# Moving the first load of the output projection ahead of the first K load in a one-token decode layer

## The chip, the cores and the metric

The kernel runs on one core of a Trainium2 chip. The core has five engines that run side by side and meet only through semaphores: TensorE (PE, matrix products; its weight loads are listed as PEld), VectorE (DVE), ScalarE (ACT), GpSimd (POOL) and SyncE (SP), which here issues all the loads. Sixteen DMA engines move the data between the chip's memory (HBM) and the core's own memory (SBUF).

The metric is the device time of one execution in microseconds (us), lower is better. A time that is quoted without more is the median of several executions. The profile is of one execution; its span is the stretch from the first to the last instruction of the program, and a little time lies around it.

## What is computed

One token goes through an attention layer with cached keys and values and then through a gated MLP, each with a layer norm in front and a residual sum behind. The batch is 1, the model width 640, there are 32 heads of width 128 and 4096 cached positions. All arrays are bf16.

```python
def _A_ref(x, k_cache, v_cache, wq, wo):
    q = (x @ wq)                                # 640 -> 32 heads x 128
    scores = einsum("bhqd,bhkd->bhqk", q, k) * (Dh ** -0.5)
    p = _softmax(scores, axis=-1)               # over 4096 positions
    o = einsum("bhqk,bhkd->bhqd", p, v)
    return o.reshape(B, Sq, Hq * Dh) @ wo       # 4096 -> 640

def _B_ref(x, w_gate, w_up, w_down):
    h = _gelu(x @ w_gate) * (x @ w_up)          # 640 -> 1728
    return h @ w_down                           # 1728 -> 640

h = x + _A_ref(_layernorm(x), k_cache, v_cache, wq, wo)
return h + _B_ref(_layernorm(h), w_gate, w_up, w_down)
```

With one token every number that is read is used once. K and V are 32 MB each (32 x 4096 x 128 x 2 bytes), wq and wo 5.2 MB each, the MLP's weights 6.6 MB: the 84 MB of the page.

## The kernel before

**Pairs.** The 32 heads are handled as 16 pairs, numbered n = 0 to 15. The K rows of a pair are one load of 2048 KB into one of three buffers (`kt`), the V rows one load of 2048 KB into one of three buffers (`vt`). I call them K0 to K15 and V0 to V15.

**PE's work for a pair.** K comes with positions on the partitions, so PE first transposes it: 64 transposes of 128x128 (`pe_transposes`, L230 to L248, matmuls of L244) in eight groups. VectorE and ScalarE copy six and two of the groups out of PSUM into `ksb` (L581 and L551). Then come 64 small products of the transposed K with q (`pe_scores`, L253). ScalarE takes the exponentials and their sums (L564). The product with V (`pe_pv`, L264, 64 matmuls) follows one pair later: in pair n's turn PE does the transposes of n, PV of n - 1, and the scores of n. Five turns of three pairs are a loop on PE (L352 to L377); pair 0 comes before it.

**The start.** SP issues the load of K0, then waits (L523), then issues x and the five parts of wq. PE transposes x (L312), computes the moments of the layer norm (L293), transposes K0, computes q from wq (L327, one part of wq after the other), brings q into columns (L343), and does the scores of pair 0.

**The output projection.** wo is 4096x640 and is used in four groups of eight heads (four pairs), 1280 KB each. A group is loaded into `wo_in` (`load_wo`, L515 to L519). POOL copies it from there into `wo` (L494) when PE has finished the projection that reads the group before; the projection runs in the second pair of each turn (L361 to L365, matmuls of L276). The turns before the first group is complete run the same projection with a row of zeros (`o_row`) against `wo`; so `wo` is cleared at the start (L481 and L483), in two parts, and PE waits for all the clears once, ahead of its loop (L349). The last group is used out of `wo_in` directly, after the loop (L406).

**SP's order of loads.** All loads go out on one queue, in the order in which SP issues them: K0, [wait], x, wq (five parts), K1, V0, and then for n = 1 to 14 K(n+1) and V(n), and V15. Ahead of V5, V8 and V11 it issues groups 0, 1 and 2 of wo, behind V15 group 3, and then the MLP's weights. SP waits ahead of a K load until PE has transposed the pair that last used the buffer (L505), ahead of a V load until the PV of the pair that last used it is done (L511), and ahead of groups 1, 2 and 3 of wo until POOL has copied the group before (L517).

**The wait at the start.** POOL counts its clears on the semaphore `pool`. The first part of `wo` is the eighth. SP waits for a count of 8 (`POOL_BEGUN`, L523) before it issues x and wq. The data of `wo` is not needed by these loads.

**The end.** Behind the loop PE does the last PV, the last projection, the moments of the second layer norm (L293), the gate and up products (L439, 140 matmuls), and the down product (L413) in the order in which the parts of w_down land. A wait of PE for a landing is L168 (`landed`).

Of the kernel before, what the change touches and what calls it, by code (L numbers as in the profile page):

```python
# [10 lines left out]
def kernel(  # L11
# [20 lines left out]
    PE, DVE, ACT, SP, POOL = nc.tensor, nc.vector, nc.scalar, nc.sync, nc.gpsimd  # L32
# [31 lines left out]
    pool = ctx.enter_context(tc.tile_pool(name="all", bufs=1))  # L64
    psum = ctx.enter_context(tc.tile_pool(name="ps", bufs=1, space=bass.MemoryType.PSUM))

    def sb(name, shape, dtype=f32):
        return pool.tile(shape, dtype, name=name, tag=name)
# [4 lines left out]
    wo_t = sb("wo", [P, HG, D], bf16)  # L73
# [74 lines left out]
    S = {n: nc.alloc_semaphore(f"s_{n}") for n in names}  # L148
# [7 lines left out]
    def spare(engine):  # L156

        i = next(spares)
        return engine.memset(spare_t[:, i : i + 1], 0.0)
# [186 lines left out]
    pe_scores(q_sb[:, 0:2], mark_at(0))  # L346
    PE.sem_inc(S["dve_pe"], -N_DVE_T)
    PE.sem_inc(S["act_pe"], -len(ON_ACT) - 1)
    PE.wait_ge(S["pool"], 9)  # L349

    base = done["pe"]
    with PE.Fori(0, TURNS):  # L352
# [28 lines left out]
    def pe_at(n, name):  # L381


        if n == 0:
            return T[0, name]
        turn, i = divmod(n - 1, UN)
        return T[("turn", i), name] + turn * per_turn
# [90 lines left out]
        POOL.memset(e[:], 0.0).then_inc(S["pool"], 1)  # L478
    POOL.memset(o_row[:], 0.0).then_inc(S["pool"], 1)
    POOL.memset(o_spread[:], 0.0).then_inc(S["pool"], 1)  # L480
    POOL.memset(wo_t[:, 0:2], 0.0).then_inc(S["pool"], 1)  # L481
    POOL_BEGUN = 8
    POOL.memset(wo_t[:, 2:], 0.0).then_inc(S["pool"], 1)  # L483

    for _ in range(2):
        spare(POOL).then_inc(S["wo"], 1)
    POOL.wait_ge(S["pe"], T["start", "q"])
    POOL.memset(wd_sb[0 : P - LAST, FULL, :], 0.0).then_inc(S["pool"], 1)
    POOL_COPIED = 10
    for g in range(NP // PG - 1):  # L490
        POOL.wait_ge(S["wo_in"], 16)
        POOL.sem_inc(S["wo_in"], -16)  # L492
# [2 lines left out]
        spare(POOL).then_inc(S["pool"], 1)  # L495
    POOL_ALL = POOL_COPIED + NP // PG - 1

    def load(name, dst, src):  # L500
        SP.dma_start(dst, src).then_inc(S[name], 16)

    def load_k(n):
        if n >= UN:
            SP.wait_ge(S["pe"], pe_at(n - UN, ("T", NG - 1)))  # L505
        src = A_k_cache[0, 2 * n : 2 * n + 2].rearrange("h (p j) d -> (h p) j d", p=HP)
        load(f"k{n % UN}", kt[n % UN][:], src)

    def load_v(n):
        if n >= UN:  # L510
            SP.wait_ge(S["pe"], pe_at(n - UN + 1, "pv"))  # L511
        src = A_v_cache[0, 2 * n : 2 * n + 2].rearrange("h (p j) d -> (h p) j d", p=HP)
        load(f"v{n % UN}", vt[n % UN][:], src)

    def load_wo(g):  # L515
        if g > 0:
            SP.wait_ge(S["pool"], POOL_COPIED + g)  # L517
        src = A_wo[g * HG * P : (g + 1) * HG * P, :].rearrange("(p j) d -> p j d", p=P)
        load("wo_in", wo_in[:], src)  # L519

    load_k(0)

    SP.wait_ge(S["pool"], POOL_BEGUN)  # L523
    load("x", x_row[:], A_x[0, 0].rearrange("(c p) -> c p", p=P))
    for c in range(DC):
        load(f"wq{c}", wq_sb[:, c, :], A_wq[c * P : (c + 1) * P, :])
# [2 lines left out]
    for n in range(1, NP):  # L529
        if n + 1 < NP:  # L530
            load_k(n + 1)
        if n in (5, 8, 11):
            load_wo((n - 5) // UN)
        load_v(n)
    load_wo(NP // PG - 1)
# [82 lines left out]
    for turn in range(TURNS):  # L618
# [14 lines left out]
        for i in range(UN):  # L633
            n = first + i
# [90 lines left out]
```

## Time and profile before

| | |
|---|---|
| time, median of 4 runs | 208.59 us (208.52 to 208.73) |
| the profiled execution: its own time | 208.73 us |
| the profiled execution: its span | 206.9 us |
| mean granted clock of PE over the span | 0.734 |
| read from HBM | 84.23 MB, 407 GB/s over the span |
| PE, share of the span that it is busy | 81% |
| DVE, ACT, POOL | 41%, 23%, 10% |
| issue of K0 | 0.95 us |
| issue of x, of the last part of wq, of K1 | 3.44, about 5.7, 6.21 us |
| issue of wo's group 0, of V5 | 56.94, 58.16 us |
| POOL's clears of `wo` | 2.24 to 3.41 and 3.35 to 6.66 us |

The page has a row of digits for each engine: the span is cut in 40 slices, and a digit is the busy share of a slice in tenths. PEclk is the clock that TensorE was granted, and below it stand the share of the DMA engines and the GB/s that they moved. In rows of the timeline the first two numbers are the start and the length in us, then come the engine, the line of the kernel, the operation, the tiles (out<-in) and how many such instructions are merged; in brackets stands how long the engine sat idle before and what ended that. "PEq L168" there means that PE's sequencer was waiting for a landing. In the table of waits a row is: who waited, for whom, us in total, how many times, the longest.

### The profile page before, as it was taken

Reading aid. Unit: us, or ns where it says so; the run is one execution under the profiler, and the core shown is the slowest. Engines: PE = TensorE matmul, PEld = TensorE weight load, DVE = VectorE, ACT = ScalarE, POOL = GpSimd, SP = SyncE. Lnnn points to the kernel's source line nnn. Section 1 sums busy time; section 2 is a strip of 40 time slices with the busy share of each in tenths; the row PEclk is TensorE's granted clock in tenths of the full one; section 3 lists DMA queues with packets and bytes.
Section 4 is the critical chain, followed back from the end, with each engine's and each line's share of the span. In section 5 each row is a group of like instructions: output and inputs, shape, how many; then the busy total and the mean of one; then the engine's idle time right before and its main releaser. Section 6 shows DMA issues by size and latency. Waiting matters only on the chain. (4 is left out here: it accounts for less than half of the span.)

```text
span 206.9 us, 7741 instructions
## 1 busy us (share of the span) xinstructions
PE 167.8 (81%) x3599; PEld 162.1 (78%) x3599; DVE 85.2 (41%) x199; ACT 48.4 (23%) x99; POOL 19.8 (10%) x22
## 2 busy tenths in 40 slices
PE   0296699795999988689899589998489899986883
PEld 0282599795999987689899589998489799984881
DVE  7492253341536607045524335252416261614330
ACT  0041132311313513032313113132213131310000
POOL 8200100000000006200003500000800000000000
PEclk9999558585679987859685856696967976765555
DMA  6999999999999999999999999999999999999990
GB/s 203 407 431 436 428 428 421 423 424 431 415 437 418 437 415 443 415 439 418 431 419 433 437 418 440 421 425 427 431 431 424 437 418 440 417 407 414 405 350 20
DMA packets 7789, 84.39 MB, mean 408 GB/s; under 512 B 802, under 2 KB 994, under 8 KB 2402
## 3 DMA queue, kind: packets, MB, share of 16 engines
q1 hardware_dynamic: 7778, 84.24, 96.9%
q8 instruction: 8, 0.13, 0.3%
q14 instruction: 3, 0.02, 0.0%
HBM read 84.23 MB, written 0.00 MB: 407 GB/s over the span
## 5 line engine op out<-in xcount | busy, mean ns | idle before, releaser
L244 PE MATMUL tp<-ident,kt 128*128 128x128 bf16 x1024 | 89.3, 272 | 8.3 <-PEq L168 7.4
L244 PEld LDWEIGHTS tp<-ident,kt 128*128 128x128 bf16 x1024 | 86.8, 127 | 9.2 <-issue 8.6
L581 DVE COPY ksb<-tp 128x1024 bf16<-128x1024 bf16 x96 | 63.8, 688 | 59.9 <-PE tp L244 59.6
L551 ACT COPY ksb<-tp 128x1024 bf16<-128x1024 bf16 x32 | 32.4, 1012 | 49.7 <-PE tp L244 49.7
L264 PE MATMUL o<-ex,vt 128*128 128x2 bf16 x1024 | 28.1, 163 | 8.0 <-PEq L168 8.0
L264 PEld LDWEIGHTS o<-ex,vt 128*128 128x128 bf16 x1024 | 27.4, 97 | 8.4 <-issue 8.4
L253 PE MATMUL s<-q,ksb 128*128 128x2 bf16 x960 | 27.0, 164 | 2.4 <-issue 2.4
L253 PEld LDWEIGHTS s<-q,ksb 128*128 128x128 bf16 x960 | 25.9, 99 | 2.5 <-issue 2.5
L494 POOL COPY wo<-wo_in 128x5120 bf16<-128x5120 bf16 x3 | 13.4, 4451 | 111.3 <-POOLq L492 111.3
L564 ACT ACTIVATE ex<-s 64x64 bf16<-64x64 f32 x32 | 7.6, 238 | 67.8 <-PE s L253 67.4
L643 DVE COPY o_raw<-o 128x2 f32<-128x2 f32 x15 | 2.4, 159 | 24.6 <-PE o L264 24.6
L439 PEld LDWEIGHTS tp<-hc,big 128*128 128x128 bf16 x140 | 8.2, 156 | 1.6 <-issue 1.6
L439 PE MATMUL tp<-hc,big 128*128 128x1 bf16 x140 | 8.3, 196 | 1.4 <-issue 1.4
L312 PE MATMUL m<-ident,x_row 5*128 5x5 bf16 x1 | 0.2, 160 | 8.7 <-PEq L168 8.7
L312 PEld LDWEIGHTS m<-ident,x_row 5*128 5x128 bf16 x1 | 0.1, 100 | 8.7 <-issue 8.7
L564 ACT ACTIVATION_READ_ACCUMULATOR ex<-s 64x1 f32 x32 | 6.4, 200 | 0.4
L276 PE MATMUL a<-o_row,wo 128*128 128x1 bf16 x200 | 5.7, 163 | 0.0
L276 PEld LDWEIGHTS a<-o_row,wo 128*128 128x128 bf16 x200 | 5.5, 96 | 0.0
L192 DVE CAST ident_f<-ident 128x128 f32<-128x128 bf16 x1 | 4.6, 4598 | 0.0
L551 ACT ACT_TABLE_LOAD x1 | 1.3, 1283 | 12.6 <-DVE rs_y L211 12.6
L327 PE MATMUL s<-big,xn_bf 128*1 128x512 bf16 x20 | 1.9, 378 | 2.5 <-PEq L168 2.5
L327 PEld LDWEIGHTS s<-big,xn_bf 128*1 128x1 bf16 x20 | 0.5, 81 | 4.1 <-issue 3.9
(97 smaller groups left out, 51.6 us busy)
## 6 DMA issues: line engine op xcount, KB each, us to landing
kt<-in_A_k_cache_dram SPq DMA_DIRECT2D x16, 2048.0 KB, 26.5
vt<-in_A_v_cache_dram SPq DMA_DIRECT2D x16, 2048.0 KB, 29.2
big<-in_A_wq_dram SPq DMA_DIRECT2D x5, 1024.0 KB, 11.3
wo_in<-in_A_wo_dram SPq DMA_DIRECT2D x4, 1280.0 KB, 26.3
big<-in_B_w_gate_dram SPq DMA_DIRECT2D x1, 2160.0 KB, 29.6
big<-in_B_w_up_dram SPq DMA_DIRECT2D x1, 1296.0 KB, 32.5
big<-in_B_w_down_dram SPq DMA_DIRECT2D x1, 1280.0 KB, 15.7
big<-in_B_w_up_dram SPq DMA_DIRECT2D x2, 432.0 KB, 19.9
```

The source lines that it names most:

```text
L192: dve(lambda: DVE.tensor_copy(ident_f[:], ident[:]), False)
L244: inst = PE.transpose(tp_b[g % NBANK][:, b * DH : (b + 1) * DH], kt[slot][:, g * GRP + b, :], ident[:])
L253: inst = PE.matmul(s_ps[:, j, :], lhsT=ksb[g][:, b * DH : (b + 1) * DH], rhs=q2, start=True, stop=True,)
L264: inst = PE.matmul(o_bank[:, 2 * region : 2 * region + 2], lhsT=vt[slot][:, j, :], rhs=e_t[slot][:, j, :], start=(j == 0), stop=(j == NB - 1),
L276: inst = PE.matmul(attn_ps[:, m : m + 1], lhsT=w[:, j, m * P : (m + 1) * P], rhs=o_row[:, j : j + 1], start=False, stop=last and j == HG - ...
L327: inst = PE.matmul(qr_ps[b][32 * r : 32 * r + 1, :], lhsT=xn_bf[:, c : c + 1], rhs=wq_sb[:, c, h * DH : (h + 4) * DH], start=False, stop=( ...
L439: inst = PE.matmul(ps[:, c : c + 1], lhsT=w[:, j, columns(c)], rhs=hc[:, j : j + 1], start=(j == 0 and c == 0), stop=(j == DC - 1), skip_g ...
L494: POOL.tensor_copy(wo_t[:], wo_in[:]).then_inc(S["wo"], 1)
L551: ACT.copy(ksb[g][:], tp_b[g % NBANK][:]).then_inc(S["act_pe"], 1)
L564: inst = ACT.activation(e_t[n % UN][r, :, i], s_ps[r, :, i], AF.Exp, scale=SCALE, accum_out=rs_all[r, 2 * n + i : 2 * n + i + 1],)
L581: DVE.tensor_copy(ksb[g][:], tp_b[g % NBANK][:]).then_inc(S["dve_pe"], 1)
L643: event(DVE.tensor_copy(o_raw[:, 2 * n - 2 : 2 * n], o_bank[:, 2 * i : 2 * i + 2]))
```

## The change

SP issues group 0 of wo first of all, then K0, x and wq, with no wait between them. The load of group 0 that stood ahead of V5 is gone from there; groups 1, 2 and 3 stay. As nothing waits for the first part of the clear any more, POOL clears `wo` in one instruction, and the counts on `pool` that PE and SP wait for are one lower. The work on PE, DVE and ACT and its order are the same.

```diff
@@ PE, ahead of the loop
-    PE.wait_ge(S["pool"], 9)
+    PE.wait_ge(S["pool"], 8)
@@ POOL
-    POOL.memset(wo_t[:, 0:2], 0.0).then_inc(S["pool"], 1)
-    POOL_BEGUN = 8
-    POOL.memset(wo_t[:, 2:], 0.0).then_inc(S["pool"], 1)
+    POOL.memset(wo_t[:], 0.0).then_inc(S["pool"], 1)
...
-    POOL_COPIED = 10
+    POOL_COPIED = 9
@@ SP
+    load_wo(0)
     load_k(0)
-
-    SP.wait_ge(S["pool"], POOL_BEGUN)
     load("x", x_row[:], A_x[0, 0].rearrange("(c p) -> c p", p=P))
     for c in range(DC):
         load(f"wq{c}", wq_sb[:, c, :], A_wq[c * P : (c + 1) * P, :])
@@ SP, in the loop over the pairs
-        if n in (5, 8, 11):
+        if n in (8, 11):
             load_wo((n - 5) // UN)
         load_v(n)
```

## The prediction

> **What bounds the kernel now.** I read the page first, its slices before its totals. PE is busy for most of the span, but at a clock that goes between half and full; the row that does not vary is the DMA row.
>
> ```profile
> span 206.9 us, 7741 instructions
> PE 167.8 (81%) x3599; PEld 162.1 (78%) x3599; DVE 85.2 (41%) x199; ACT 48.4 (23%) x99; POOL 19.8 (10%) x22
> ...
> DMA  6999999999999999999999999999999999999990
> GB/s 203 407 431 436 428 428 421 423 424 431 415 437 418 437 415 443 415 439 418 431 419 433 437 418 440 421 425 427 431 431 424 437 418 440 417 407 414 405 350 20
> ...
> q1 hardware_dynamic: 7778, 84.24, 96.9%
> ```
>
> The reader is to see one queue, q1, that moves 84.24 MB, is at work in every slice but the first and the last, and keeps 415 to 440 GB/s. At 427 GB/s (the window table's figure for 20 to 60 us) 84.24 MB take 197.3 us of the 206.9. So the time is: when the stream starts, how many bytes it has, whether it is ever empty, and what is left to do behind its last byte.
>
> Next I read who waits at the end, PE's timeline from 188 us on:
>
> ```profile
> 192.06 8.25 PE L439 MATMUL tp<-hc,big 128*128 128x1 bf16 x140 [1.42 <-issue]
> ...
> 200.66 0.30 PE L413 MATMUL tp<-big,hid 128*1 128x160 bf16 x4 [0.35 <-PEq L168]
> 201.35 1.24 PE L413 MATMUL tp<-big,hid 128*1 128x160 bf16 x32 [0.38 <-PEq L168]
> 202.88 0.83 PE L413 MATMUL tp<-big,hid 128*1 128x160 bf16 x20 [0.29 <-PEq L168]
> ```
>
> L168 is where PE waits for a landing. The last matmuls wait three times, 1.02 us in all: the final parts of w_down set the end, and PE alone would be at most about 1 us earlier. From the last matmul (203.71) to the span's end it is 3.2 us of copy, store and closing, which the change does not touch.
>
> Then SyncE's own waits, for what the removed wait holds back:
>
> ```profile
> SPq L501 <- POOL wo L481: 2.1, 1, 2.1
> ```
>
> Last, PE around the place that wo's first group leaves:
>
> ```profile
> 76.54 5.22 PE L244 MATMUL tp<-ident,kt 128*128 128x128 bf16 x64 [0.56 <-PEq L168]
> 84.67 1.75 PE L264 MATMUL o<-ex,vt 128*128 128x2 bf16 x64 [2.90 <-PEq L168]
> 86.28 1.83 PE L253 MATMUL s<-q,ksb 128*128 128x2 bf16 x64
> 87.97 0.57 PE L375 MATMUL m<-rs_cur,ones_f 128*128 128x8 f32 x2
> 89.41 5.60 PE L244 MATMUL tp<-ident,kt 128*128 128x128 bf16 x64 [0.87 <-PEq L168]
> ```
>
> K6 landed at 76.5, V5 at 84.6, K7 at 89.4. Between 76.54 and 89.41 three loads landed, 1280 + 2048 + 2048 = 5376 KB in 12.87 us. So a 2048 KB load takes 4.90 us of the stream and a group of wo 3.06 us.
>
> **The change, part by part.**
>
> *The wait removed (SP, 2.1 us).* Behind it stood x and the five wq loads (x issued at 3.44 instead of about 1.35). Do they land sooner? x lands at 8.7 (PE's first matmul, 8.71, waits on L168), only when K0 in front of it has gone through, and wq follows at the stream's rate (wq3 at 18.66, wq4 at 21.14: 2.48 us for 1024 KB). The queue was not empty between 3.4 and 8.7; K0's transfer hides the wait. Gain 0.
>
> *The load moved.* wo's first group (1280 KB, one DMA, issue 0.44 us) goes from behind K6 to the head of SP's order, past 18 issues: K0 to K6, V0 to V4, x and five of wq. Everything it passes lands 3.06 us later; everything from V5 on has the same bytes in front of it as before. Bytes, DMA count and the first issue (0.95 us) stay. If the stream starts equally well, its end stays: 0.
>
> *PE's delay.* x, K0, wq, K1 and K2 land 3.06 later, so PE's first transposes begin near 12.9 instead of 9.80, those of K1 near 29.1 (26.04 + 3.06) and those of K2 near 40.4 (37.37 + 3.06). From K2's transposes to pair 6's PE waits for no load until 75.98; 75.98 - 37.37 = 38.6 us, so PE would be ready for K6 at 79.0, and K6 lands at 79.6. Its transposes end after 5.2 us, at 84.8, when V5 (84.6) is already there. From 84.67 to the end of the totals PE needs 3.87 us, so it is ready for K7 at about 88.7, and K7 lands at 89.4 as before. The 2.90 us wait ahead of PV5 becomes a wait ahead of K6, and the delay is gone by pair 7, with 0.7 us over. Were pair 6's transposes at half clock (6.43 us, the row at 50.11, against 5.22) PE would be 0.5 us late at K7, and the next waits (0.98 us ahead of K8, 2.11 ahead of PV8) take that up. After 89.4 PE has 9.3 us of such waits. Cost 0.
>
> *SP and the buffers.* K3's issue waits for K0's transposes: 16.27 becomes about 19.4. It lands near 50, with K2 and V1 ahead of it in the queue, and the page's median from issue to landing is 26.5 us for kt and 29.2 for vt; 3 us of 26 are cover enough. Cost 0; without that cover, 3 us.
>
> *POOL.* Two clears of wo (1.17 and 3.31 us) become one of about 4.4; PE's wait on it (8 instead of 9) comes at about 29 us, long after 6.7. The first copy of wo_in (4.45 us) no longer waits for the load (79.66) but for pair 5's projection (72.78 + 3.1 = 75.9), so wo's second load is not held back any more: SP's two waits on that copy were 3.3 us, none of which emptied the queue. Four DVE evictions beside the copy took 2.63 us, 0.66 each, against 0.69 without it: no contention. 0.
>
> *The start of the stream.* This is the one term that the trace of before doesn't price. In the window table by single microseconds the stream moves 49, 229, 279 and 393 GB/s in the four from 1 to 5 us; up to 9.0 us it moves 2.58 MB, which is 6.05 us at 427. So 2.95 us are lost: 1.97 before the first packet, 0.98 in a ramp. In the packet records the first packets (16 KB) of K0 took 0.96 to 1.75 us, later ones 0.61, and K0's parts land over 0.77 us (7.85 to 8.62), a spread that later loads keep. The new head has 10 KB packets, and nine more issues follow without a pause. From below: if the ramp goes by packets, 6/16 of 0.98 = 0.37 us are saved, and of the spread 6/16 of 0.77 = 0.29, together -0.6. From above: the ramp is doubled, +1.0. If it goes by time, 0. I take 0, as most of the first packets took over 1 us and the size cannot be told apart here.
>
> Sum: 208.73 (the profiled execution: span 206.9 and 1.8 around it) + 0. The median of the four runs is 208.59, 0.14 lower; I forecast against it: 208.6.
>
> *Rules.* After that sum, two places of the Trainium skill. "DMA: Bandwidth & Descriptors", Anatomy of one DMA, gives a DMA (of the GpSimd path) a fixed cost of about 2.0 us beside bytes / 436 GB/s. By it wo's group would delay K0 by 5.0 us, not 3.06, an estimate against the change. The row above (12.87 us for three loads) leaves no room for fixed costs between queued loads. "TensorE: Matmul & The Clock Gate", Part 1, says that the clock is throttled by default and that activity releases it. The table grants 1.00 from 0 to 20 us with PE busy for 9.09 of 20, and 0.50 from 22 to 30 with PE busy for 6.84 of 8. By the rule the busy catch-up after 40 us would run at full clock; I count it at the clock of its rows.
>
> **The rivals.**
>
> 1. *The start suffers (slower).* The wait also keeps SP from issuing while the engines are starting: only K0's descriptors are there until 3.44. Now wo, K0, x and wq are issued from 0.95 to about 4.3, across the whole ramp (1.97 to 3.9). If that makes it half as long again or twice as long, the end moves by 0.5 to 1.0 us: 209.1 to 209.6, centre 209.3. It decides from a loss above 0.4 us. For it: one engine began its first packet only at 2.89, so the start is uneven. Against it: no row shows issues and packets in each other's way later.
>
> 2. *The start gains (faster).* 10 KB first packets and the smaller spread, -0.4 to -0.6: 208.1. For it: the last landing sets the end, and a late engine stays late. Against it: a slow start may be one of time.
>
> 3. *PE doesn't catch up (slower).* It would have to lose 9.3 us more in waits, or run T2 to T15 at half clock. Beyond that, each us is a us: 210 or more. Against it: the working above.
>
> 4. *It moves 3 us of waiting and nothing else.* This is the forecast.
>
> **How the numbers follow.** The measurement tells about 0.2% from no change, 0.42 us. Forecast, 208.2 to 209.0: 0.43. Rival 1: 0.30. Rival 3: 0.04. Rival 2: 0.23. The range takes in both ends of the start, 208.59 - 0.6 - 0.1 = 207.9 and 208.59 + 1.0 = 209.6, and leaves rival 3 and the far ends of the others out. The forecast's own range is 208.2 to 209.0.
>
> **What would show it.** In the profile after: PE's first matmul near 11.8; transposes of K1 near 29.1; a wait of 2.5 to 3.5 us on L168 ahead of pair 6's transposes and none ahead of its PV; K7's transposes again at 89.4 within 0.5; the last matmuls still with waits on L168. If K7 comes at another time by x, the start of the stream has moved by x, and I expect the end to move with it; the first slices' GB/s say by which rival. If K7's wait on L168 is gone and PE is late from there on, it is rival 3. An empty queue anywhere (a slice under 400 GB/s between 10 and 185 us) would make the whole reading wrong.

## The result and the profile after

| | before | after |
|---|---|---|
| time, median | 208.64 us (60 runs) | 208.27 us (40 runs) |
| ratio, 95% interval | | 0.9983 (0.9978 to 0.9987) |
| the profiled execution: its own time | 208.73 us | 208.31 us |
| the profiled execution: its span | 206.9 us | 206.5 us |

The change makes the kernel faster by 0.37 us, 0.17%. That is small, but nearly four times the half-width of the interval. The forecast was no change; a gain of 0.4 to 0.6 us stood there as rival 2.

The rows of the page that answer to those of before:

```profile
span 206.5 us, 7740 instructions
PE 168.3 (81%) x3599; PEld 162.6 (79%) x3599; DVE 85.3 (41%) x199; ACT 48.4 (23%) x99; POOL 19.8 (10%) x21
...
DMA  5999999999999999999999999999999999999990
GB/s 198 446 413 422 451 409 441 411 435 409 438 419 425 428 435 425 428 427 425 428 422 438 425 428 428 428 424 426 435 425 435 422 428 425 428 406 414 407 360 24
...
q1 hardware_dynamic: 7778, 84.24, 96.8%
```

The bytes are the same, and again there is no empty slice. The first slice is lower than before (198 against 203) and the second higher (446 against 407): a slice is 5.17 us, too coarse for what follows. By single microseconds the window table gives 2.70 MB up to 9.0 us, against 2.58 MB before. Three rows of PE's timeline of the kernel before, to compare with:

```profile
8.71 0.16 PE L312 MATMUL m<-ident,x_row 5*128 5x5 bf16 x1 [8.71 <-PEq L168]
...
26.04 6.52 PE L244 MATMUL tp<-ident,kt 128*128 128x128 bf16 x64 [0.21 <-PEq L168]
...
37.37 6.00 PE L244 MATMUL tp<-ident,kt 128*128 128x128 bf16 x64 [1.53 <-PEq L168]
```

PE's timeline of the kernel after, from its start to the place in the middle and then the end:

```profile
11.51 0.16 PE L312 MATMUL m<-ident,x_row 5*128 5x5 bf16 x1 [11.51 <-PEq L168]
...
28.80 5.15 PE L244 MATMUL tp<-ident,kt 128*128 128x128 bf16 x64 [0.20 <-PEq L168]
...
40.05 6.29 PE L244 MATMUL tp<-ident,kt 128*128 128x128 bf16 x64 [1.10 <-PEq L168]
...
79.20 5.36 PE L244 MATMUL tp<-ident,kt 128*128 128x128 bf16 x64
84.40 1.75 PE L264 MATMUL o<-ex,vt 128*128 128x2 bf16 x64
86.00 1.74 PE L253 MATMUL s<-q,ksb 128*128 128x2 bf16 x64
87.61 0.37 PE L375 MATMUL m<-rs_cur,ones_f 128*128 128x8 f32 x2
88.99 5.36 PE L244 MATMUL tp<-ident,kt 128*128 128x128 bf16 x64 [1.02 <-PEq L168]
...
200.21 0.30 PE L413 MATMUL tp<-big,hid 128*1 128x160 bf16 x4 [0.35 <-PEq L168]
200.93 1.23 PE L413 MATMUL tp<-big,hid 128*1 128x160 bf16 x32 [0.42 <-PEq L168]
202.45 0.84 PE L413 MATMUL tp<-big,hid 128*1 128x160 bf16 x20 [0.29 <-PEq L168]
```

The reader is to compare the starts with those of before. The first matmul is 2.80 us later (11.51 for 8.71), not 3.06; K1's transposes are 2.76 us later (28.80 for 26.04), K2's 2.68 (40.05 for 37.37); K7's transposes come 0.42 us earlier (88.99 for 89.41) with a wait on the landing in both; the last matmuls come 0.43 us earlier (202.45 for 202.88) and still wait for w_down. So the first landing that PE waits for comes 0.26 us earlier than the forecast has it, and the end has gained what K7 has gained.

**The landing records.** For a load into 128 partitions the trace has 16 increments of its semaphore, one per DMA engine, here called landings; each engine has eight packets of such a load. Counted from the first packet of the queue, the last landing of the last load (the last part of w_down, wd3) is at 201.19 us before and 200.74 after. The profiled executions' own times are 7.54 and 7.57 us later, and the same difference is 7.53 to 7.59 in 16 of the 18 profiles of this study (7.80 and 7.87 in e5 and e6). So the time of this kernel is the last landing of wd3 and about 7.56 us.

K1's landings tell the start. Two numbers serve below: the **start loss**, which is the mean of K1's 16 landings less the time that one engine's packets up to there take at their steady durations (0.611 us for 16 KB, 0.385 for 10 KB, 0.309 for 8 KB, so 16 x 0.611 + 40 x 0.309 = 22.14 us for K0, wq and K1), and the **spread**, last less first of the 16.

| | start loss | spread at K1 |
|---|---|---|
| before | 1.56 us | 0.74 us |
| after | 1.34 us | 0.34 us |

What was gained at the start stays. Less the bytes that it has more or less ahead of it, the mean landing is 0.22 us earlier than before at K1, and 0.22 or 0.23 at K7, K15 and V15; for wd3 it is 0.32, and no run shows what the last 0.1 us is. The last of wd3's 16 landings lies 1.11 us behind their mean before and 0.99 after, so the end moved by 0.32 + 0.12 = 0.44 us (0.45 by the rounded times above).

The first packets show where it comes from. Here are six of the first for each kernel (start from the queue's first packet, size, duration):

```
before  0.00 16 KB 1.10   0.06 16 KB 1.53   0.13 16 KB 1.70   0.42 16 KB 1.60   0.92 16 KB 0.86   0.99 16 KB 1.42
after   0.00 10 KB 1.08   0.06 10 KB 1.27   0.08 10 KB 1.23   0.73 10 KB 0.67   0.85 10 KB 0.52   1.07 10 KB 0.39
```

Before, some engines have their first packet done after 1.0 us and others after 2.0, and several second packets are slow too. After, eight packets begin at once and the next eight 0.7 to 1.1 us later, all of these are done by about 1.5 us, and from then on packets take their steady time.

### The profile page after: what moved, and what is told of

Read it like the earlier page. It is cut to its first block, busy times and chain, and to the rows that moved or that the text cites. A ratio compares the mean times of both kernels' runs of the same rounds, so it can differ in the third digit from the quotient of the medians.

```text
span 206.5 us, 7740 instructions
## 1 busy us (share of the span) xinstructions
PE 168.3 (81%) x3599; PEld 162.6 (79%) x3599; DVE 85.3 (41%) x199; ACT 48.4 (23%) x99; POOL 19.8 (10%) x21
## 5 line engine op out<-in xcount | busy, mean ns | idle before, releaser
L244 PE MATMUL tp<-ident,kt 128*128 128x128 bf16 x1024 | 90.3, 274 | 7.2 <-PEq L168 6.6
L244 PEld LDWEIGHTS tp<-ident,kt 128*128 128x128 bf16 x1024 | 87.7, 128 | 8.2 <-issue 7.2
L481 POOL MEMSET wo<- 128x5120 bf16 x1 | 4.4, 4373 | 0.0
```

The costliest lines, as they stand in the source:

```text
L244: inst = PE.transpose(tp_b[g % NBANK][:, b * DH : (b + 1) * DH], kt[slot][:, g * GRP + b, :], ident[:])
L481: POOL.memset(wo_t[:], 0.0).then_inc(S["pool"], 1)
```

## The experiments

The gain could have three causes: the wait that is gone (B), the group's place in the middle (C), and the start of the stream by the first load (A); within A it could be the packets' size or something else in that load. "Ratio" is the time over that of the kernel before, measured beside it. "Start loss" and "spread" are from the one profiled execution of each program.

**e1, the wait alone.** `SP.wait_ge(S["pool"], POOL_BEGUN)` is taken out of the kernel before.

> The kernel before without SP's wait; wo's first group stays ahead of V5, K0 is the first load. Theory A (the size of the first packets sets how far apart the 16 engines start, and the last engine sets the end): K0's 16 KB packets are first as before, so K0's parts land over about 0.8 us as before and the time stays, ratio 0.999 to 1.001. Theory B (the wait's removal made the gain): the spread falls to about 0.4 us and the ratio is 0.998 or less. Theory C (the group's place in the middle matters): ratio 1.000.

Measured: ratio 1.0006 (0.9997 to 1.0015), start loss 1.57, spread 1.09. The wait is worth nothing in time. B falls.

**e2, the move alone.**

```diff
+    load_wo(0)
     load_k(0)
     SP.wait_ge(S["pool"], POOL_BEGUN)
...
-        if n in (5, 8, 11):
+        if n in (8, 11):
```

> wo's first group is first and K0 second, as in the kernel after, but SP's wait stands behind K0 again, ahead of x. Theory A: spread of the first load about 0.4 us, ratio about 0.998. Theory B: no gain, ratio 1.000, spread about 0.8 us. Theory C: ratio about 0.998.

Measured: 0.9985 (0.9976 to 0.9994), start loss 1.36, spread 0.32. It has the whole gain, with the wait still there.

**e3, the group early but not first.** `load_wo(0)` stands behind `load_v(0)`, and not ahead of V5.

> K0 first and SP's wait as before; only wo's first group goes from ahead of V5 to behind V0, early but not first. Theory A: K0's packets start the stream as before, spread about 0.8 us, ratio 0.999 to 1.001. Theory B: 1.000. Theory C (what counts is that PE no longer has the 2.9 us wait in the middle): ratio about 0.998.

Measured: 0.9999 (0.9990 to 1.0008), start loss 1.50, spread 0.84. C falls: taking the group out of the middle gains nothing. It has to be the head of the queue.

**e4, nothing moved, K0 in halves.**

```diff
-    landed("k0")
+    PE.wait_ge(S["k0"], 32)
+    PE.sem_inc(S["k0"], -32)
...
-    load_k(0)
+    half = A_k_cache[0, 0:2].rearrange("h (p j) d -> (h p) j d", p=HP)
+    for i in range(2):
+        part = slice(i * NB // 2, (i + 1) * NB // 2)
+        load("k0", kt[0][:, part, :], half[:, part, :])
```

> The kernel before with K0 loaded by two loads of 1024 KB, so that the first packets have 8 KB in place of 16; wo and the wait as before. Theory A: the spread falls to 0.4 us or less and the ratio to about 0.998, with nothing moved. Theories B and C: ratio 1.000.

Measured: 0.9978 (0.9969 to 0.9987), start loss 1.28, spread 0.75. This has the gain of the change without the change: PE's first matmul is at 8.76, so K0 is not delayed. But the spread, by which theory A explains the gain, did not fall (0.75 against 0.74); the start loss did. The end is earlier all the same:

```profile
200.31 1.67 PE L414 MATMUL tp<-big,hid 128*1 128x160 bf16 x36 [0.35 <-PEq L168]
202.28 0.84 PE L414 MATMUL tp<-big,hid 128*1 128x160 bf16 x20 [0.31 <-PEq L168]
```

These rows of PE's timeline of e4 are the last matmuls, 0.60 us earlier than before and still behind landings.

**e5, K0 in quarters (4 KB packets).**

> The kernel before with K0 in four loads of 512 KB, packets of 4 KB. Theory A2 (each engine's first one or two packets take about 0.5 to 1.1 us longer the more bytes they have, so the size of the first packets sets what the start costs): at least the gain of 8 KB packets, ratio 0.9965 to 0.998; mean of the 16 engines' landings of K0 0.2 to 0.4 us earlier than before. Rival D (what counts is that a second load is queued early, not the packet's size): ratio about 0.998, no better than halves. Rival E (a slow start of fixed time, 8 KB was luck): ratio 0.999 to 1.001.

Measured: 1.0058 (1.0045 to 1.0072), start loss 1.78, spread 1.02. None of the three theories has this; it is the opposite of what "smaller is better" (A2) asks for. A part of it is the packets themselves: four of 4 KB take 0.636 us, one of 16 KB 0.611, so K0 takes 0.20 us more.

**e6, K0 by heads (two loads of 64 partitions).**

> K0 in two loads of 1024 KB like the halves, but cut by head: 64 partitions each, packets of 16 KB as before. Theory A2: no gain, ratio 0.999 to 1.001. Rival D: the gain of the halves, about 0.998.

Measured: 1.0219 (1.0206 to 1.0233). It does not test what it was made for, as its page shows about half the rate in the second slice and more than 400 only from the fourth on:

```profile
GB/s 149 217 290 425 436 427 427 419 424 427 427 421 427 427 423 437 421 436 422 424 437 423 427 433 427 424 433 422 429 430 427 430 427 430 430 404 414 402 362 20
```

**e7, the kernel after with wo's group in two halves (5 KB packets).**

> The kernel after with wo's first group in two loads of 640 KB, packets of 5 KB in place of 10. Theory A2: 0.1 to 0.3 us better than the kernel after, ratio 0.997 to 0.998. Rival D and rival E: as the kernel after, 0.998 to 0.9985.

Measured: 0.9990 (0.9981 to 0.9999), start loss 1.58, spread 0.93. That is no better than the kernel after (0.9983) and outside what A2 forecast, though the intervals of the two overlap. The profiled execution (208.77 us) was the slowest of its runs (median 208.37), so its start loss is rather high for this program.

**e8, K0 as a quarter of 4 KB packets and three quarters of 12 KB.**

> K0 in two loads: first a quarter with 4 KB packets, then three quarters with 12 KB packets. Theory A2: as only the first packets of each engine are slow, the gain is that of the quarters, ratio 0.9965 to 0.998. If the packets of all of K0 mattered, the gain would be smaller than that of the halves, 0.998 to 0.9995.

Measured: 1.0022 (1.0013 to 1.0031), start loss 1.67, spread 1.01. It is slower than before, which neither expectation has.

**e9, K0 cut 40 + 24 blocks (10 and 6 KB); e10, 48 + 16 (12 and 4 KB).**

> The kernel before with K0 in two loads, first 40 of its 64 blocks (packets of 10 KB, as wo's), then 24 (6 KB); nothing moved. Theory A3 (what the start costs depends on the size of the first packets and is least near 8 to 10 KB; the tensor does not matter): as the kernel after, ratio 0.9975 to 0.999. Rival F (wo's rows are what starts well, not their size; the halves had another reason): 0.9995 to 1.001.

> The same with 48 blocks (12 KB) and then 16 (4 KB). Theory A3: between 10 and 16 KB, ratio 0.9985 to 1.0005. Rival F: 1.000 to 1.002 (more, smaller packets).

Measured: e9 1.0026 (1.0016 to 1.0036), start loss 1.62, spread 0.74; e10 1.0019 (1.0010 to 1.0028), start loss 1.91, spread 0.60. Both are slower, e9 by more than rival F has too. With packets of wo's size, cut out of K0, the start is not wo's start (1.62 against 1.34). Theory A3, that the size alone decides, fails in e9. The start does not carry all of e9's time either: the mean of wd3's landings is where it was before, but the last of the 16 is 0.37 us later. One engine is 1.75 us behind the mean in the first load of w_up, against 1.26 before; why is open.

**e11, wq's first part at the head (8 KB packets), wo left in the middle.**

```diff
+    load("wq0", wq_sb[:, 0, :], A_wq[0:P, :])
     load_k(0)
...
-    for c in range(DC):
+    for c in range(1, DC):
```

> The kernel before with the first part of wq (1024 KB, packets of 8 KB, contiguous) ahead of K0; wo stays ahead of V5. Theory A3: the start of the halves, mean start loss about 1.3 us in place of 1.56, ratio 0.9975 to 0.9985. Rival F: 1.000.

Measured: 0.9982 (0.9973 to 0.9991), start loss 1.18, spread 0.28. That is as theory A3 has it, and rival F falls: wo is not needed for the gain at all.

**e12, the kernel after once more.**

> The kernel after once more, for a second profile of the same program beside these. Spread of K1's landings over the engines 0.3 to 0.4 us and ratio 0.998 to 0.9985, if one profile stands for the program's start; if the spread is a matter of chance it comes out elsewhere between 0.3 and 1.1 us.

Measured: 0.9979 (0.9970 to 0.9988), start loss 1.29, spread 0.57. The loss comes back within 0.05 us, the spread does not (0.34 before): a spread from one profile is partly chance, a start loss much less so.

**e13 to e16, a needless load at the head.** To part size, tensor and gaps, a load that nothing uses goes ahead of K0, into a V buffer that is free then; this is the edit of e13, and in the others the source and the size differ:

```diff
-    landed("k0")
+    PE.wait_ge(S["k0"], 32)
+    PE.sem_inc(S["k0"], -32)
...
+    room = vt[2][:].rearrange("p j d -> p (j d)")[:, 0:8192]
+    load("k0", room, A_wq[0 : 2 * P, :].rearrange("(p r) n -> p (r n)", r=2))
     load_k(0)
```

> The kernel before with one needless load ahead of K0: 256 rows of wq (2048 KB, one whole stretch of memory) in packets of 16 KB into a buffer that is free then; K0 waits for both. The result is the reference's. Its bytes alone cost 4.90 us: 208.6 + 4.9 = 213.5. Theory S (the first packets' size decides): start as before, spread of K1 over the engines 0.6 us or more, 213.3 to 213.7. Theory T (the K tensor starts badly, wq and wo well): spread 0.4 or less, 212.9 to 213.2. Theory G (a whole stretch in packets of at most 10 KB starts well): as theory S.

> The same with 1024 KB of K's first head, one whole stretch, packets of 8 KB. Its bytes alone cost 2.47 us: 211.1. Theories S and G: spread 0.4 us or less, 210.6 to 210.9. Theory T: spread 0.6 or more, 211.0 to 211.3.

> The same with every second row of the first 256 of wq: packets of 8 KB from addresses 16 KB apart, 1024 KB. Bytes alone: 211.1. Theories S and T: spread 0.4 us or less, 210.6 to 210.9. Theory G (gaps between the packets spoil it): spread 0.6 or more, 211.0 to 211.3.

> The same with the first 128 rows of wq, one whole stretch, packets of 8 KB; the yardstick for the other three. All theories: spread 0.4 us or less, 210.6 to 210.9.

| head of the queue | packets | time, us | less its bytes | start loss | spread at K1 |
|---|---|---|---|---|---|
| e13, wq, whole stretch | 16 KB | 213.46 | 208.6 | 1.58 | 0.70 |
| e14, K, whole stretch | 8 KB | 210.73 | 208.3 | 1.24 | 0.48 |
| e15, wq, every second row | 8 KB | 210.51 | 208.0 | 1.26 | 0.69 |
| e16, wq, whole stretch | 8 KB | 210.64 | 208.2 | 1.27 | 0.50 |

The time of the bytes is 4.90 us in e13 and 2.47 in the others. Each was run four times, and the interval of its time is about 0.35 us either way, so the start loss has to carry the comparison. It goes with the size and not with the tensor: wq in 16 KB packets starts as badly as K0 (1.58 and 1.56), K in 8 KB packets as well as wq (1.24 and 1.27). Gaps between 8 KB packets cost nothing that shows in time or start loss (e15). The spread came out above the expected 0.4 us in all three with 8 KB; as e12 says, it is the weaker sign. The first microseconds show the difference, e13 and then e14, in the window table (start:end, length, busy time of PE, PEld, DVE, ACT, POOL, clock, DMA share, GB/s):

```profile
2.00:3.00 1.00, 0.00 (x0) 0.00 (x0) 1.00 (x2) 0.00 (x0) 1.00 (x4) 1.00 1.47 262
3.00:4.00 1.00, 0.00 (x0) 0.00 (x0) 1.00 (x1) 0.00 (x0) 1.00 (x2) 1.00 0.67 246
4.00:5.00 1.00, 0.00 (x0) 0.00 (x0) 1.00 (x1) 0.00 (x0) 1.00 (x1) 1.00 0.96 410
```

```profile
2.00:3.00 1.00, 0.00 (x0) 0.00 (x0) 1.00 (x2) 0.00 (x0) 1.00 (x4) 1.00 0.46 131
3.00:4.00 1.00, 0.00 (x0) 0.00 (x0) 1.00 (x1) 0.00 (x0) 1.00 (x2) 1.00 1.00 418
4.00:5.00 1.00, 0.00 (x0) 0.00 (x0) 1.00 (x1) 0.00 (x0) 1.00 (x1) 1.00 1.04 442
```

The table books a packet whole in the window in which it starts, so 262 and 131 are both 16 packets. In the next microsecond only 15 packets of 16 KB start (246), but 51 of 8 KB (418): with 8 KB packets the queue is at its full rate from 3 us on, with 16 KB only from 4 us on (410).

**What is settled and what is open.** Settled: the gain is in the start of the queue and depends on which load is its head; the wait, the place in the middle and the tensor are not it. Heads with 16 KB packets lost 1.50 to 1.58 us (four profiles: before, e1, e3, e13; e6 is left out, as it ran at half the rate). Heads with 8 KB packets, or with wo's whole 10 KB rows, lost 1.18 to 1.36 (eight profiles). Open: why heads of 4, 5, 10 and 12 KB packets that were cut out of longer rows lost 1.58 to 1.91 (five), when 8 KB cut out of 16 KB did not (e4). All five have the rest of the row in further loads right behind, but so has e4. Open too is why a first packet of 16 KB takes longer than its steady time by more than one of 8 KB does: the trace has its start and its duration, and no cause.

## Why the prediction was wrong

- *"If the stream starts equally well, its end stays" and "K7 by x, the end by x".* Right: K7 came 0.42 us earlier, the last matmul 0.43.
- *"I take 0" for the start.* This is the step that failed: a term of the sum was put at 0 that measured -0.37 us. The bounds of -0.6 and +1.0 hold it. There were two readings, a cost by packets and one by time, and time was chosen because most of the first packets took over 1 us; e16 against e13 shows that the size does count: with the same tensor 1.27 against 1.58 us are lost.
- *Rival 2, the start gains.* It had the way and the place right, and its terms too large. For the ramp it had 0.37 us; the start loss fell by 0.22 (1.56 to 1.34) and 0.27 (e12). For the spread it had 0.29; the spread at K1 fell (0.74 to 0.34, and 0.57 in e12), but at wd3 it is 2.27 before and 2.25 and 2.24 after, and the last landing is nearer to the mean by 0.12 and 0.20 us only. What widens the spread on the way is told below. Its reason, "10 KB first packets", is half right: 8 KB starts better than 16 KB, but smaller is not better as a rule (e5, e8 to e10). And the ramp of 0.98 us was read from the window table, which books a packet whole where it starts; by the landings the start lost 1.56.
- *The wait removed, gain 0.* Right (e1).
- *Rival 1, the start suffers from the issues that the wait kept back.* Wrong: e1 has no wait and keeps the start loss (1.57), e2 has the wait and the gain.
- *PE's delay, cost 0.* Right in sum: K1's transposes start at 28.80 (29.1 forecast), K2's at 40.05 (40.4), and PE has caught up at K7. One sign was wrong: a wait of 2.5 to 3.5 us ahead of pair 6. It did not fit the working, which left 0.6 us; in the trace there is none, since PE comes to pair 6 at 79.13 instead of 79.0 and K6 lands at 79.1 instead of 79.6. The 3.46 us that PE waited there before are simply used up by the late start.
- *SP and POOL, 0.* Right. K3 is issued at 19.30 (19.4 forecast); the first copy of `wo_in` runs at 75.98 (75.9). SP was held up while issuing K2 and V1 (1.41 and 2.70 us in place of about 0.45), with no empty queue behind it.
- *The fixed cost of a DMA in the Trainium skill ("DMA: Bandwidth & Descriptors", Anatomy of one DMA), by which K0 would be delayed by 5.0 us.* The first matmul moved by 2.80 us. The page gives the cost for the GpSimd path; the loads here, queued from SP, paid no such cost one by one.
- *The clock, "1.00 from 0 to 20 us".* This was a wrong reading. The trace's first record of the clock is at 14.8 us, and the table counts time without a record as full. PE's 32 transposes from 9.80 on took 3.57 us, 112 ns each; the 64 from 68.07 on, where the clock is recorded at 1.00, took 3.73 us, 58 ns each. So the first transposes ran at about half speed, and what the prediction draws from the 1.00 does not stand. No term of the sum rests on it.

## What to carry to other kernels

Where one queue is busy from the first microsecond to the last, look at its two ends: at what lands last, engine by engine, and at what its first packets are. What stands in the middle of the order could move by tens of microseconds here and change nothing (e3, 0.9999), while another load at the head of the queue was worth 0.2%. Halving the head load's packets (e4, 0.9978) gained as much as the move, without delaying anything; the three good heads (wo, half of K0, wq's first part) cannot be told apart by their intervals. So try it, and do not assume that smaller is better: quarters of K0 cost 0.6% (e5).

## What the hardware showed beyond that

- **Each instruction read makes one engine late, and it stays late.** The trace has eight packets of 16 KB on the instruction queue (q8), about 1.1 us each, the first at 26.1 us before. K1, ahead of it, landed over 0.74 us; V0, behind it, over 2.29, one engine being 1.5 us later, and 2.27 is still the spread at wd3. K2 has two late landings (by 1.4 and 1.6 us behind the mean) behind two reads, V1 four behind four, one of which is a read of 8 KB on q14. The late engines do not catch up: at K5, behind six of the reads, seven of the 16 landings are 0.4 to 1.2 us behind their mean, and at V15, 117 us later, it is seven by 0.3 to 1.2. "Runtime: NRT & Kernel Launch", Instruction fetch mechanics, in the Trainium skill says that instructions are refilled in blocks of 16 KiB on a queue of the sequencer's own and that this is mostly hidden. The blocks agree; but for a load that waits for its slowest engine they are not hidden.
- **A load into 64 partitions ran at half the rate.** In e6 K0, cut into two loads of 64 partitions each, took until 11.3 us after the first packet (6.7 before), at 217 GB/s in the second slice, and its packets of 16 KB took 1.28 us instead of 0.61. "SBUF — State Buffer", Door 1, in the Trainium skill says that partitions 0 to 63 reach only half of the DMA ports. That agrees.
